# Weight matrices through GpSimd's transfer queue, late stores through SyncE's, in a gated linear attention with a max-of-three feed-forward layer

## The chip, the cores and the metric

The kernel runs on one core of a Trainium2 chip. The metric is the device time of one execution in microseconds. Engines are named as in the profile: PE (TensorE matmuls; PEld its weight loads), DVE (VectorE), ACT (ScalarE), POOL (GpSimd) and SP (SyncE). Three of them can issue transfers between memory and the on-chip buffer: SP, ACT and POOL; a transfer is then run by the core's 16 DMA engines. Each engine runs its own instructions in program order.

## The reference

```python
# q, k, v, alpha: (4, 8, 768, 48); w1, w2, w3: (384, 768); w_out: (768, 384)
for t in range(S):
    state = alpha[:, :, t, :, None] * state + np.einsum('bhd,bhe->bhde', k[:, :, t], v[:, :, t])
    y[:, :, t] = np.einsum('bhd,bhde->bhe', q[:, :, t], state)
x = y.transpose(0, 2, 1, 3).reshape(B * S, H * D)          # (3072, 384)
h = np.maximum(np.maximum(x @ w1, x @ w2), x @ w3)
out = h @ w_out                                            # (3072, 384), float32
```

## The kernel before

The sequence of 768 steps is cut into 6 blocks of 128. A **unit** u is one block of one of the 4 batches, with all 8 heads: 24 units, in the order block by block. Two units make a **pair** n (12 pairs): q, k, v and alpha are loaded for a pair at a time, or for one unit of it ("half loads", 192 KB) in pairs 0, 1 and 3.

For each unit, `decay` takes the logarithm of alpha on ACT (L509); `prep` sums it along the block on PE (L562), takes exp of plus and minus the sum on ACT (`ep`, `en`, L565 and L567), multiplies q and k by these on POOL or DVE (L574, by the table `EARLY`), scales v (L586), transposes q and k (on PE, L544, copied out by DVE, L548; from unit `CROSS_IN` on by a transfer of SP, L593), and computes scores (L608) that DVE masks (`LA`, L613). `output` multiplies the scores by v and the carried state by q (L654, L651), scales the result into `xb` on ACT (L662) and transposes it to `xT` (on PE, L676, copied by DVE, L680; from unit `CROSS_OUT` on by a transfer of SP). `state` carries the state to the next block (L706, L712, L719).

The feed-forward layer uses max(a, b, c) = a + max(0, b − a, c − a). With w1 as the base, `subs` computes `wd` = w2 − w1 and w3 − w1 in 16 bits (L456). For a group f of one or two units, `ffn` runs six (or four) pieces: x·wd on PE (L747), relu for the first matrix on ACT (L758), maximum for the second on DVE (L763). The output is h·w_out plus x·(w1·w_out) (L780); the product w1·w_out, `w1o`, is made once: `turned` transposes w1 on PE (L474) with copies on ACT (L480), and `folded` multiplies it by w_out (L491). That product is called the **fold** here. Groups 0 and 1 are single units (`SINGLE`), the others two units. Each finished unit is copied out of PSUM by ACT (L791) and stored by ACT's queue (L792).

The order is not that of the source: each step is handed to a planner (`Plan`) with its engine, a cost, a rank, what it reads and writes; `order` simulates the engines, the transfer queues and the PSUM banks and emits the steps engine by engine in the order found. Two lists stand outside of that: SP issues its loads in the order of `FIRST`, and then pair by pair, in one line ("loads"). In the kernel before, `FIRST` holds the weights too, in column parts of 512 and 256 (`WCUTS`), so SP's one queue brings both; `wload` (L437) lands w1 and w_out as 32-bit numbers in a staging buffer that they share (`ws0`), and ACT casts them to 16 bits (L447). `WARM` names zero matmuls on PE that stand beside the startup; before, their count is 0.

## Time and profile before

| | |
|---|---|
| three runs | 153.97, 154.49 (median), 156.53 us |
| profiled execution | 154.55 us, span 152.8 us, granted PE clock 1.00 |
| PE busy | 132.5 us (87%) |
| DVE, ACT, POOL busy | 97.7, 86.7, 66.7 us |
| transfers by SP's queue | 24.74 MB, 76.8% of 16 engines' span |
| transfers by ACT's queue | 4.72 MB, 9.1% |
| read from memory, written | 23.69 MB, 4.72 MB |

The span is the time from the first to the last instruction; the execution's own time is 1.75 us longer. "Busy" leaves out waits and the issuing of transfers. In the windows, each row is a stretch of the span: its bounds and length, then busy time and number of instructions of PE, PEld, DVE, ACT and POOL, the granted clock, the mean share of the 16 DMA engines, and GB/s. In the chain of waits each row is start, length and what the end of the program hung on then; a DMA in it is a wait for a transfer, from its issue to its landing. In the timeline a row is start, length, engine, line, operation and tiles, with the idle time ahead of it and what ended that in brackets.

### The profile page before, as it was taken

The page shows a single profiled execution, that of the slowest core. Times are in us where ns is not written, and L with a number is a line of the kernel's source. Part 1 is how long each engine was busy: PE and PEld are TensorE (multiplying, and loading weights), DVE is VectorE, ACT ScalarE, POOL GpSimd, SP SyncE. Part 2 cuts the span into 40 slices and gives each one's busy share as a digit, 9 for nine tenths or more (in the row PEclk, how much of TensorE's full clock was granted, in tenths as well). Part 3 has the DMA queues.
Part 4 walks back from the last instruction along what each step waited for, and adds up shares of the span by engine and source line. Part 5 has one row for each costly group of instructions (what it writes and reads, how often), then busy time and mean ns, then how long its engine had stood idle before and what let it go on. Part 6 is the DMA issues. An engine that isn't in the chain of part 4 may idle for free.

```text
span 152.8 us, 4049 instructions
## 1 busy us (share of the span) xinstructions
PE 132.5 (87%) x1616; PEld 104.4 (68%) x1616; DVE 97.7 (64%) x172; ACT 86.7 (57%) x173; POOL 66.7 (44%) x95
## 2 busy tenths in 40 slices
PE   0416458689999999999999999999999999999990
PEld 0205237558877887798697788698697878778760
DVE  7025552878793699988686799587874482385230
ACT  3706556658626785777748567568395426336211
POOL 0223107010721143587978589496999910000000
PEclk9999999999999999999999999999999999999999
DMA  6999998999799999999999979999999706020113
GB/s 121 203 275 195 283 342 186 375 221 238 162 230 206 274 235 193 241 263 197 223 245 219 230 174 221 193 282 180 257 213 221 193 4 172 0 101 6 66 37 103
DMA packets 110578, 29.71 MB, mean 194 GB/s; under 512 B 104160, under 2 KB 109408, under 8 KB 110560
## 3 DMA queue, kind: packets, MB, share of 16 engines
q1 hardware_dynamic: 106816, 24.74, 76.8%
q10 hardware_dynamic: 3744, 4.72, 9.1%
q8 instruction: 12, 0.20, 0.5%
q14 instruction: 6, 0.05, 0.1%
HBM read 23.69 MB, written 4.72 MB: 186 GB/s over the span
## 4 chain that ended last, share of the span: by engine, by line
PE 77%; SPq 11%; DMA 7%; ACT 2%; issue 1%; ACTq 0%
PE psum L747 30%; PE psum L780 23%; SPq L415 10%; PE psum L544 5%; DMA ws<-in_moe_w_out_dram 4%; PE psum L608 4%; DMA ws<-in_moe_w_dram 3%; PE psum L654 3%; PE psum L676 2%; PE psum L562 2%; PE psum L651 2%; PE psum L706 2%; PE psum L491 2%; PE psum L522 1%; ACT wo L447 1%
## 5 line engine op out<-in xcount | busy, mean ns | idle before, releaser
L747 PE MATMUL psum<-xT,wd 128*128 128x256 f16 (+1 forms) x468 | 55.5, 270 | 1.6 <-DVE xT L680 1.6
L747 PEld LDWEIGHTS <-wd 128*128 128x128 f16 x468 | 42.4, 101 | 7.1 <-DVE wd L456 1.6
L613 DVE TENSOR_TENSOR LA<-psum,c 128x1024 f16<-128x1024 f32 x24 | 28.6, 1219 | 7.7 <-PE psum L608 7.5
L758 ACT ACTIVATE hT<-psum 128x512 f16<-128x512 f32 (+1 forms) x37 | 21.5, 588 | 16.8 <-PE psum L747 15.9
L763 DVE TENSOR_TENSOR hT<-psum,hT 128x512 f16<-128x512 f32 (+1 forms) x37 | 24.5, 673 | 9.5 <-PE psum L747 9.3
L574 POOL TENSOR_TENSOR qk<-qn,ep 128x384 f16<-128x384 f32 x18 | 18.0, 998 | 23.0 <-ACT ep L565 12.8
L780 PE MATMUL psum<-wo,hT 128*128 128x384 f16 x144 | 27.3, 326 | 0.0
L791 ACT COPY ob<-psum 128x384 f32<-128x384 f32 x23 | 11.0, 479 | 18.8 <-PE psum L780 18.6
L574 POOL TENSOR_TENSOR qk<-kn,en 128x384 f16<-128x384 f32 x19 | 19.3, 1020 | 2.9 <-DMA kn<-in_k_dram 2.8
L780 PEld LDWEIGHTS <-hT 128*128 128x128 f16 x144 | 14.1, 98 | 9.3
L586 POOL TENSOR_SCALAR v<-vn,c 128x384 f16<-128x384 f32 x21 | 12.6, 602 | 17.4 <-DMA vn<-in_v_dram 17.3
L719 POOL TENSOR_TENSOR Z<-U,G 48x192 f16<-48x192 f32 x32 | 15.8, 502 | 9.0 <-DVE U L712 7.8
L662 ACT ACTIVATE xb<-psum,c 128x384 f16<-128x384 f32 x24 | 13.7, 581 | 6.7 <-PE psum L654 3.2
L548 DVE COPY qkT<-psum 128x1024 f16<-128x1024 f16 x20 | 13.6, 687 | 5.8 <-PE psum L544 5.7
L544 PE MATMUL psum<-c,qk 128*128 128x128 f16 x160 | 13.1, 228 | 3.5 <-POOL qk L574 3.5
L780 PE MATMUL psum<-w1o,xT 128*128 128x384 f16 x72 | 15.6, 326 | 0.0
L680 DVE COPY xT<-psum 128x384 f16<-128x384 f16 x24 | 8.3, 354 | 9.8 <-PE psum L676 8.2
L562 PE MATMUL psum<-la,c 128*128 128x384 f16 x24 | 8.4, 351 | 6.0 <-ACT la L509 6.0
L544 PEld LDWEIGHTS <-qk 128*128 128x128 f16 x160 | 10.5, 102 | 4.1 <-POOL qk L574 3.8
L565 ACT ACTIVATE ep<-psum 128x384 f32<-128x384 f32 x24 | 11.9, 494 | 1.8 <-PE psum L562 1.5
L509 ACT ACTIVATE la<-an 128x768 f16<-128x768 f32 (+1 forms) x14 | 10.4, 746 | 3.6 <-DMA an<-in_alpha_dram 3.6
L567 ACT ACTIVATE en<-psum 128x384 f32<-128x384 f32 x24 | 11.9, 497 | 0.4 <-ACT ob L791 0.4
(41 smaller groups left out, 147.0 us busy)
## 6 DMA issues: line engine op xcount, KB each, us to landing
out_dram<-ob ACTq DMA_DIRECT2D x23, 192.0 KB, 3.0
an<-in_alpha_dram SPq DMA_DIRECT2D x10, 384.0 KB, 5.6
qn<-in_q_dram SPq DMA_DIRECT2D x9, 384.0 KB, 6.5
kn<-in_k_dram SPq DMA_DIRECT2D x9, 384.0 KB, 6.5
vn<-in_v_dram SPq DMA_DIRECT2D x9, 384.0 KB, 6.0
ws<-in_moe_w_dram SPq DMA_DIRECT2D x3, 768.0 KB, 6.6
qn<-in_q_dram SPq DMA_DIRECT2D x6, 192.0 KB, 4.5
kn<-in_k_dram SPq DMA_DIRECT2D x6, 192.0 KB, 4.6
```

What stands on the lines that cost most here:

```text
L415: nc.sync.dma_start(t[:, lo:hi], views[x][cb * P:(cb + 1) * P, g * HG + lo:g * HG + hi])
L544: nc.tensor.transpose(live[tk][:, w, j, :], qk[:, w, 2 * j:2 * j + 2, :], ident)
L548: plan.step("DVE", 0.69, u, lambda: nc.vector.tensor_copy(out=qkT, in_=live[tk]), reads=[tk], writes=[("qkT", u % 3)])
L574: nc.gpsimd if eng == "POOL" else nc.vector).tensor_mul(
L586: lambda: nc.gpsimd.tensor_scalar(out=v16, in0=ld["v"][n % 5][:, hs], scalar1=vsc, scalar2=1.0, op0=AOP.mult, op1=AOP.mult),
L613: lambda: nc.vector.tensor_mul(LA.rearrange("p a b t -> p (a b) t"), live[Ak].rearrange("p a (b t) -> p (a b) t", t=P), maskA.unsqueeze(1) ...
L662: lambda: nc.scalar.activation(out=xb, in_=live[yk].rearrange("p a b -> p (a b)"), func=AFT.Copy, scale=ysc),
L719: eng.tensor_mul(Zn[rows, :, cols], U[rows, :, cols], G[rows, i * NP:(i + 1) * NP].unsqueeze(2).broadcast_to([D, NP, D]))
L747: nc.tensor.matmul(live[gk][:, jj, :], wd[:, kt, g, j * P:(j + 1) * P], xT[:, kt, :], start=(kt == 0), stop=(kt == NFT - 1))
L758: lambda h=h, gk=gk: nc.scalar.activation(out=h, in_=live[gk], func=AFT.Relu),
L763: lambda h=h, gk=gk: nc.vector.tensor_max(h, live[gk], h),
L780: nc.tensor.matmul(live[ok], a[:, i * P:(i + 1) * P], w, start=(kt == 0), stop=(kt == nk - 1))
```

## The change

The four weight matrices leave SP's list. POOL issues one transfer for each whole matrix (`weights`): w1 and w_out arrive as 16-bit numbers in `w1h` and `wo16`, cast by the transfer; w2 and w3 arrive as 32-bit numbers. `WPOOL` says behind what each is issued: w1 at the start, w2 when v of unit 0 is scaled, w3 and w_out when v of unit 1 is. The staging buffer and ACT's four casts are gone. The subtractions all run on DVE. Stores of units 16 to 22 are issued by SP instead of ACT (`LEAVE`). xT of units 18 to 23 is made by SP's transposing transfer (`CROSS_OUT` 24 to 18), and qk of unit 20 is transposed by PE again (`CROSS_IN` 20 to 21). 18 zero matmuls stand in the startup (`WARM`). The tables of the planner, `EARLY`, `LEAD`, `FIRST` and the queue constants are new, so that the order of all engines is another.

In the order that comes out, PE's first steps are: the sum for unit 1 (from here on lines are those of the changed kernel; L588), the 18 transpositions of w1 (L500), the sum for unit 0, the transpositions and scores of units 1 and 0; then 72 matmuls of the feed-forward groups 0 and 1 (L773, with qk of unit 3 in between), scores of unit 3, 12 matmuls of the fold (L517), qk of unit 2, the output of unit 3, and the last 6 of the fold. POOL's first steps are: the transfer of w1 (L467), k and q of unit 1, v of unit 0, q of unit 0, the transfer of w2, v of units 2 and 1, the transfers of w3 and w_out. SP's list begins with alpha and k of unit 1, alpha of unit 0, q of both, v and k of unit 0 and v of unit 2; then come k of units 2 and 3, alpha of unit 2 and, as the twelfth half load, v of unit 1.

```diff
--- before.py
+++ after.py
@@ -23,29 +23,29 @@
 HOP = {"PE": 0.25, "ACT": 0.1, "DVE": 0.1, "POOL": 0.1, "SP": 0.0}
 TURN_RANK, TURN_COST = 2.0, 0.1
 SP_FIRST = 0.9
-QUEUES = ("SP", "ACT")
-DMA_IN = {"SP": 0.9, "ACT": 0.9}
-DMA_OUT = {"SP": 0.9, "ACT": 0.9}
-DMA_BOTH = {"SP": 0.17, "ACT": 0.8}
-LANES, LANES_USED, LANDING = {"SP": 6, "ACT": 99}, 2, 2.4
+QUEUES = ("SP", "POOL")
+DMA_IN = {"SP": 0.9, "POOL": 2.7}
+DMA_OUT = {"SP": 0.9, "POOL": 0.9}
+DMA_BOTH = {"SP": 0.15, "POOL": 0.85}
+LANES, LANES_USED, LANDING = 6, 2, 2.4
 SPARE = 1.5
-LEAD = (9.0, 6.5, 2.0, 7.5)
-EARLY = {0: ("DVE", "DVE", "POOL"), 2: ("POOL", "DVE", "POOL"), 3: ("DVE", "DVE", "POOL"),
-         4: ("DVE", "POOL", "POOL"), 6: ("DVE", "DVE", "ACT"), 8: ("POOL", "POOL", "ACT"),
-         9: ("DVE", "DVE", "ACT"), 11: ("DVE", "POOL", "POOL")}
+LEAD = (8.0, 8.5, 2.0, 8.5)
+EARLY = {0: ("POOL", "DVE", "POOL"), 1: ("POOL", "POOL", "POOL"), 3: ("DVE", "POOL", "POOL"),
+         4: ("POOL", "POOL", "POOL"), 5: ("DVE", "POOL", "POOL"), 6: ("POOL", "POOL", "POOL"),
+         7: ("DVE", "POOL", "POOL"), 8: ("POOL", "DVE", "POOL"), 11: ("POOL", "POOL", "POOL")}
 WCUTS = (0, 512, 768)
-SUBS = {(1, 0): "DVE", (1, 1): "POOL", (2, 0): "DVE", (2, 1): "DVE"}
-FIRST = (("a", 0, 1, 2), ("a", 0, 0, 1), ("q", 0, 1, 2), ("k", 1, 0, 1), ("q", 0, 0, 1),
-         ("k", 0, 1, 2), ("w", 0, 0), ("v", 1, 0, 1), ("v", 0, 0, 1), ("k", 0, 0, 1),
-         ("k", 1, 1, 2), ("a", 1, 0, 1), ("w", 0, 1), ("v", 0, 1, 2), ("w", 1, 0), ("w", 1, 1),
-         ("w", 3, 1), ("aq", 1, 1, 2), ("q", 1, 0, 1), ("w", 3, 0), ("w", 2, 0), ("w", 2, 1),
-         ("v", 1, 1, 2), ("aqkv", 2, 0, 2), ("k", 3, 0, 1), ("a", 3, 0, 2), ("v", 3, 1, 2),
-         ("q", 3, 0, 1), ("v", 3, 0, 1), ("q", 3, 1, 2), ("k", 3, 1, 2))
-WARM = (-1, 1, 0)
-BACK, WQUEUE, WTAX = 1, "SP", 0.1
+SUBS = {(1, 0): "DVE", (1, 1): "DVE", (2, 0): "DVE", (2, 1): "DVE", (2, 2): "DVE",
+        (1, 2): "DVE"}
+FIRST = (("a", 0, 1, 2), ("k", 0, 1, 2), ("a", 0, 0, 1), ("q", 0, 1, 2), ("qv", 0, 0, 1),
+         ("k", 0, 0, 1), ("v", 1, 0, 1), ("k", 1, 0, 2), ("a", 1, 0, 1), ("v", 0, 1, 2),
+         ("a", 1, 1, 2), ("q", 1, 1, 2), ("q", 1, 0, 1), ("v", 1, 1, 2), ("aqkv", 2, 0, 2),
+         ("ka", 3, 0, 1), ("a", 3, 1, 2), ("q", 3, 0, 1), ("qv", 3, 1, 2), ("k", 3, 1, 2),
+         ("v", 3, 0, 1))
+WARM = (0, 1, 18)
+WPOOL, ROWS, WTAX = {0: (), 1: (0, "v"), 2: (1, "v"), 3: (1, "v")}, False, 0.1
 SINGLE, LAST = 2, 0
 PAIRS, WIDE = 10, 99
-CROSS_IN, CROSS_OUT = 20, 24
+CROSS_IN, CROSS_OUT, LEAVE = 21, 18, 16
 FETCH, FETCHES, STORE = 0.75, (25.0, 10.2), 0.25
 CLOCK_WINDOW, CLOCK_PHASE, CLOCK_WAKE, CLOCK_KEEP = 3.413, 0.0, 0.75, 0.4
 
...
@@ -422,43 +424,67 @@
                       late=0.0 if n < 3 else SPARE)
             asked.append((x, n % 5, lo // H))
 
-    nparts = len(WCUTS) - 1
+    nparts = 3 if ROWS else len(WCUTS) - 1
     matrices = (moe_w1, moe_w2, moe_w3, moe_w_out)
-    casting = {g: tuple(x[2] for x in FIRST if x[:2] == ("w", g)) for g in (0, 3)}
+    by_sp = {g: [x[2] for x in FIRST if x[:2] == ("w", g)] for g in (0, 3)}
+    got, built = set(), []
+
+    def arranged(g, part):
+        got.add((g, part))
+        for k, (h, what) in enumerate(((0, turned), (3, folded))):
+            if len(built) == k and all((h, p) in got for p in range(nparts)):
+                built.append(h)
+                what()
 
     def piece(t, g, part):
+        if ROWS:
+            return t[:, 2 * part:2 * part + 2, :] if g == 3 else t[:, part:part + 1, :]
         lo, hi = WCUTS[part], WCUTS[part + 1]
         return t[:, lo // P:hi // P, :] if g == 3 else t[:, :, lo:hi]
 
+    def size(part):
+        return DF if ROWS else NFT * (WCUTS[part + 1] - WCUTS[part])
+
     def wload(g, part):
-        room = [("ws room", p) for p in casting[0]] if g == 3 else []
-        gate = [asked[-1 - BACK]] if len(asked) > BACK and WQUEUE == "ACT" else []
-        plan.step(WQUEUE, 0.5, -1.0,
-                  lambda: (nc.scalar if WQUEUE == "ACT" else nc.sync).dma_start(
+        plan.step("SP", 0.5, -1.0,
+                  lambda: nc.sync.dma_start(
                       piece(wst[g], g, part),
                       piece(matrices[g].rearrange("(t p) f -> p t f", p=P), g, part)),
-                  reads=gate + room, writes=[("ws", g, part)],
-                  line="weights" if WQUEUE == "ACT" else "loads",
-                  load=3.25 * (WCUTS[part + 1] - WCUTS[part]) / DF
-                  + (WTAX if WQUEUE == "SP" else 0.0))
+                  reads=[("ws room", p) for p in by_sp[0]] if g == 3 else [],
+                  writes=[("ws", g, part)], line="loads",
+                  load=(3.15 if ROWS else 3.25) * size(part) / (NFT * DF) + WTAX)
         if g in (0, 3):
-            n = NFT * (WCUTS[part + 1] - WCUTS[part])
-            plan.step("ACT", 0.2 + 0.00083 * n, -0.5,
+            plan.step("ACT", 0.2 + 0.00083 * size(part), -0.5,
                       lambda: nc.scalar.copy(out=piece((w1h, 0, 0, wo16)[g], g, part),
                                              in_=piece(wst[g], g, part)),
                       reads=[("ws", g, part)],
                       writes=[("w", g, part)] + [("ws room", part)] * (g == 0))
+            arranged(g, part)
+
+    def weights(g, gate):
+        cast = g in (0, 3)
+        plan.step("POOL", 0.78, -1.0,
+                  lambda: nc.gpsimd.dma_start((w1h, wst.get(1), wst.get(2), wo16)[g],
+                                              matrices[g].rearrange("(t p) f -> p t f", p=P)),
+                  reads=gate, writes=[("w" if cast else "ws", g, p) for p in range(nparts)],
+                  line="weights", load=3.3)
+        if cast:
+            for p in range(nparts):
+                arranged(g, p)
 
     def subs(g, part):
-        cols = slice(WCUTS[part], WCUTS[part + 1])
-        n, eng = NFT * (cols.stop - cols.start), SUBS[g, part]
-        plan.step(eng, 0.2 + n * (0.0019 if eng == "POOL" else 0.00102), 0.0 if g == 1 else 3.0,
+        eng = SUBS.get((g, part), "DVE")
+        plan.step(eng, 0.2 + size(part) * (0.0019 if eng == "POOL" else 0.00102),
+                  0.0 if g == 1 else 3.0,
                   lambda: (nc.gpsimd if eng == "POOL" else nc.vector).tensor_sub(
-                      wd[:, :, g - 1, cols], wst[g][:, :, cols], w1h[:, :, cols]),
+                      piece(wd[:, :, g - 1, :], g, part), piece(wst[g], g, part),
+                      piece(w1h, g, part)),
                   mode=int(eng == "DVE"),
                   reads=[("ws", g, part), ("w", 0, part)], writes=[("wd", g, part)])
 
     def parts_of(j):
+        if ROWS:
+            return list(range(nparts))
         return [p for p in range(nparts)
                 if WCUTS[p] < 2 * (j + 1) * P and WCUTS[p + 1] > 2 * j * P]
 
@@ -769,6 +795,7 @@
             r = rank[2 * (NJ // span) + i]
             ok = ("op", m)
             nk = NFT + NJ
+            cb, b = divmod(m, B)
             parts = [(0, nk)] if m < NU - UB else [(0, nk - span), (nk - span, nk)]
             for lo, hi in parts:
                 def shrink(i=i, ok=ok, lo=lo, hi=hi):
@@ -791,8 +818,17 @@
                 nc.scalar.copy(out=obs[m % 4], in_=live[ok])
                 nc.scalar.dma_start(out[b * S + cb * P:b * S + (cb + 1) * P, :], obs[m % 4])
 
+            if m < min(LEAVE, NU - 1):
+                plan.step("ACT", 0.86, r, leave, reads=[ok], writes=[("ob room", m % 4)], load=-STORE)
+                continue
             if m < NU - 1:
-                plan.step("ACT", 0.86, r, leave, reads=[ok], writes=[("ob room", m % 4)], load=-STORE)
+                plan.step("ACT", 0.49, r,
+                          lambda m=m, ok=ok: nc.scalar.copy(out=obs[m % 4], in_=live[ok]),
+                          reads=[ok], writes=[("ob room", m % 4), ("ob", m)])
+                plan.step("SP", 0.4, r,
+                          lambda b=b, m=m: nc.sync.dma_start(
+                              out[b * S + cb * P:b * S + (cb + 1) * P, :], obs[m % 4]),
+                          reads=[("ob", m)], writes=[("left", m)], load=-STORE)
                 continue
             left, right = slice(0, DM // 2), slice(DM // 2, DM)
             rows = out[b * S + cb * P:b * S + (cb + 1) * P, :]
@@ -816,13 +852,14 @@
     for what, n, lo, *hi in FIRST:
         if what == "w":
             wload(n, lo)
-            if n in casting and lo == casting[n][-1]:
-                turned() if n == 0 else folded()
         else:
             load(n, lo * H, hi[0] * H, what)
     if WARM[0] < 0:
         warm(*WARM)
-    made = dict.fromkeys(SUBS, False)
+    for g, gate in WPOOL.items():
+        if not gate:
+            weights(g, [])
+    made = {(g, p): False for g in (1, 2) for p in range(nparts)}
     due = []
     for n in range(NU // B):
         us = list(range(n * B, (n + 1) * B))
@@ -839,13 +876,17 @@
                 state(u)
         for u in range(n * UB, (n + 1) * UB):
             prep(u)
+            for g, gate in WPOOL.items():
+                if gate and gate[0] == u:
+                    weights(g, [("v16", u % 7) if gate[1] == "v"
+                                else ("qk", u % 7, "qk".index(gate[1]))])
             if u >= PAIRS and u % UB == 0:
                 continue
             if u == WARM[0]:
                 warm(*WARM)
             for v in (u - 1, u) if u >= PAIRS else (u,):
                 output(v)
-        for key in SUBS:
+        for key in made:
             if not made[key] and ("w", 0, 0) in plan.writer and ("ws", *key) in plan.writer:
                 made[key] = True
                 subs(*key)
```

More of the change, by code (lines that the diff above doesn't have):

```diff
@@ L232, in order @@
                         t = max(t, held["DVE" if e == "POOL" else "POOL"])
-                    if self.steps[i][6] and len(lanes) >= LANES[e]:
-                        if lanes[-LANES[e]] is None:
+                    if e == "SP" and len(lanes) >= LANES:
+                        if lanes[-LANES] is None:
                             continue
-                        t = max(t, lanes[-LANES[e]])
+                        t = max(t, lanes[-LANES])
                     turn = TURN_RANK if e == "PE" and self.steps[i][7] != mode else 0.0
@@ L248, in order @@
                 end, i = dma.next(commit=True)
-                lanes[number[i]] = end
+                if i in number:
+                    lanes[number[i]] = end
                 self.landed[i] = end
@@ L270, in order @@
                 dma.add(e, t + cost + DMA_IN[e], load, i, late)
-                number[i] = len(lanes)
-                lanes.append(None)
+                if e == "SP":
+                    number[i] = len(lanes)
+                    lanes.append(None)
             else:
```

## The prediction

> **What bounds the kernel now.** First the head of the page, for the span and the busiest engine:
>
> ```profile
> span 152.8 us, 4049 instructions
> ...
> PE 132.5 (87%) x1616; PEld 104.4 (68%) x1616; DVE 97.7 (64%) x172; ACT 86.7 (57%) x173; POOL 66.7 (44%) x95
> ```
>
> The profiled execution took 154.55 us, 1.75 more than its span; the median of the three runs, 154.49, is the same within 0.1. A measurement of this kernel can tell about 2% (3.1 us) from no change. Then the windows of 8 us, for where PE is not busy:
>
> ```profile
> 0.00:8.00 8.00, 1.76 (x14) 0.97 (x14) 3.52 (x19) 4.02 (x8) 1.20 (x5) 1.00 0.85 161
> 8.00:16.00 8.00, 3.53 (x32) 2.84 (x33) 2.78 (x5) 2.97 (x3) 2.16 (x3) 1.00 0.98 234
> 16.00:24.00 8.00, 3.82 (x41) 2.62 (x41) 4.59 (x6) 4.10 (x8) 1.83 (x2) 1.00 1.04 304
> 24.00:32.00 8.00, 6.25 (x82) 5.33 (x80) 3.79 (x6) 5.33 (x10) 1.81 (x2) 1.00 1.00 300
> 32.00:40.00 8.00, 8.00 (x108) 6.35 (x107) 6.64 (x12) 5.66 (x13) 1.93 (x2) 1.00 1.06 195
> ```
>
> From 32 us on PE is busy for all of each window up to 144; before, it idles while the DMA engines are full (DMA share near 1). So there are two stages: a startup set by transfers, and a dense stage set by PE's work. The chain of waits shows where one passes into the other:
>
> ```profile
> 23.53 6.05 DMA ws<-in_moe_w_out_dram
> ...
> 29.60 1.48 ACT wo L447
> ...
> 31.12 1.14 PE psum L491 x6
> ```
>
> The second part of w_out lands at 29.58, ACT casts it, and from 31.12, the first matmul of the fold w1·w_out, PE never waits again until its last matmul starts at 148.8. That is 117.7 us; 4.0 more are the last copies and stores. Hence time = start of the fold + dense work + 4.0 + 1.75.
>
> **What the change takes from the dense work.** In PE's new order both halves of the first two FFN groups stand ahead of the fold; now the second halves (36 matmuls of 128 columns; nine take 0.51 in the chain) come after it: −2.0. Units 18 to 23 lose the transposition of xb on PE (three matmuls, 0.17 each in the chain): −1.0. Unit 20 goes back to PE for qk (eight matmuls, 0.45): +0.45. Unit 2's qk transposition and scores (0.45, 0.23) move behind the fold: +0.7. Sum −1.9, dense work 115.8. The 18 zero matmuls (WARM) lie in the startup, where PE waits anyway; six of them, cold, are 2 us at most if that wait were gone.
>
> **When can the fold start?** Its new gate is w_out as fetched by POOL's queue, the last of four fetches. No row shows a transfer issued by POOL, so I build it from neighbours:
>
> ```profile
> 2.25 1.67 DVE L381 MEMSET Z<- 128x192 uint32 x8
> ...
> 4.15 0.52 ACT L509 ACTIVATE la<-an 128x384 f16<-128x384 f32 x1 [1.24 <-DMA an<-in_alpha_dram]
> ...
> 5.10 0.52 ACT L509 ACTIVATE la<-an 128x384 f16<-128x384 f32 x1 [0.42 <-DMA an<-in_alpha_dram]
> ...
> 7.57 0.56 DVE L574 TENSOR_TENSOR qk<-qn,ep 128x384 f16<-128x384 f32 x1 [3.65 <-DMA qn<-in_q_dram]
> ```
>
> - Loads: the first lands at 4.15, and from 5.10 to 7.57 three more land: 0.82 us per half load (one unit of a, q, k or v).
> - A weight's transfer, X: the first 768 KB of w3 let DVE start at 31.66, 2.06 after w_out had let ACT start at 29.60; a whole matrix, half as large again, 3.1. That is the lower end (nothing beside it). If loads beside it get half of the bytes, 6.2. The issue table has ACT's 192 KB stores landing in 3.0 us while SP's loads of the same size take 4.5: a second queue does not stand behind the first. So I lie near the lower end: X = 3.9.
> - Rest of issue to landing: the 96.5 KB constant on ACT's queue took 2.5 us, the 1.5 KB one 3.2; with 1.0 for POOL's own work on the issue (its instructions take 0.6 to 1.0), 4.2. Bounds 2.5 and 6.
>
> w1: issued at about 0.7, landed at 0.7 + 4.2 + 3.9 = 8.8. PE's second step in program order is the 18 transpositions of w1, so unit 0 waits behind it: six transpositions 0.75 (twelve took 1.46), ACT's copy 0.75, ln 0.52, second copy 0.75, exp 0.48, POOL's multiply 0.99, about 4.5 with the hand-overs. Only behind that multiply does POOL issue w2: 13.3, landed 21.4. w3's issue stands behind v of unit 1, the twelfth half load: 4.15 + 11·0.82 = 13.2, and 3.3 more that w1's stream takes from it: 16.5. POOL scales it (0.6) and issues w3 and w_out at about 17.3 and 18, in time to queue behind w2: w3 lands at 25.3, w_out at 29.2. So landing = 13.6 + 4X, and the fold starts at 29.4 (no cast in between).
>
> What must be there by then: wd from w3, 1.76 + 0.95 on DVE, 28.0, and its 18 last matmuls, 29.0; 0.4 is left. Next is alpha of pair 2, half loads 17 and 18: 4.15 + 17·0.82 + 4·3.3 = 31.3, ln 0.84, 32.1; PE asks for it 3.8 after the fold starts (1.95 + 0.45 + 0.2 + 0.98 + 0.23), at 33.2. It is covered by 1.1 us; a still earlier fold would wait here.
>
> **Costs taken at nothing.** ACT loses 4.6 us of casts, three scalings and seven store issues (0.34 each), all idle time now. POOL gains 3 q, 3 k and 3 v operations (7.9 us) and four issues (2.4 to 4), and loses one subtraction (2.06): about 9 us, in units 0 to 11, where it was busy 7.0 of 32 us and 5.6 of the next 16; without that cover, qk of unit 3 or 4 would be late by 1 us each. SP's queue: the xb transfers of units 22 and 23 stand behind two stores, whose copies come earlier in ACT's order; after the last attention matmul PE has 18 + 24 matmuls of 256 columns (4.6) and 18 of w_out (2.9), 7.5 us, against copy 0.58, two issues of 1.25 and landing (qkT's transfers took 3.1 to 4.1): about 6. Margin 1.4; the price without it is 1 to 2 us. The last store's right half may wait up to 0.4 for SP's store before it.
>
> **Sum:** 29.4 + 115.8 = 145.2 for PE's last matmul, span 149.2, time 151.0: 1.7 from the earlier fold, 1.9 from the dense work. With X = 3.1 and 2.5 of latency, the fold could start at 26.4, but alpha would hold PE for 1.9 more: 149.9. The other end is the third rival.
>
> **Rivals.**
> 1. *The bytes set the startup, whoever issues them.* DMA share is already 0.98 to 1.04 from 8 to 32 us, and the bytes from memory are the same. Then the fold starts where it did, 31.1, or at 32.0 if w2's stream pushes v of unit 1 (16.5 against w2's start near 17) and w3 is issued behind it. Time 31.1 + 121.55 = 152.7, to 153.6. Against it: the cast ahead of the fold (1.48) goes, and the last part of w_out took 6.05 us from issue to landing for 768 KB that need 2.1, with loads of SP ahead of it in the one queue. The Trainium skill (DMA: Bandwidth & Descriptors, section Issuing engines are not separate DMA queues) says just this, that another issuer saves only issuing time. By that rule the time is this rival's; the DMA share agrees with it.
> 2. *w1's fetch starts late.* DVE fills tiles until 3.92. If POOL's issue is held until then, everything after w1 moves by 3.2: fold 32.6, time 154.2. No POOL work stands beside those fills in the trace. The Trainium skill (SBUF — State Buffer, section SBUF: two separate sides, the box on the "DVE blocks DMA" trap) says that POOL cannot write descriptors while DVE holds the shared port; no run here shows whether a fill does.
> 3. *Slower: POOL's transfers are slow and stand one behind the other.* X counts four times, and w1 holds PE, ACT and through unit 0 the issue of w2. The fold may start 1.9 later than before, at 33.0, until nothing is gained: 13.8 + 4X = 33.0 gives X = 4.8. At X = 6.2 (loads take half, or the two casting transfers run at half rate) w_out lands at 38.4: 38.6 + 121.55 = 160.1. For it: casts by transfer are in no row. Against it: the stores' 3.0.
>
> **How the numbers follow.** Forecast 0.43 (its own range 149.5 to 151.4), rival 1 0.17, rival 2 0.12, rival 3 0.28. Over 2% faster is below 151.4: the forecast, 0.43. Rivals 1 and 2 lie within 2%: 0.29. Rival 3 is mostly past 157.6: 0.28. The range goes from 149.0, just under the floor of 149.9, to 159.0, which leaves out the far end of rival 3, some 0.15, and 0.05 below.
>
> **What would show it.** Right: w1h landed at 8 to 9.5 us, w2 issued near 13, w3 landed near 25 to 26, the fold (L517) starting at 29 to 30 and PE without a gap from there, last matmul near 145. Rival 1: landing of w_out at 31 to 32. Rival 2: w1h landed near 12 with a normal transfer. Rival 3: a weight's transfer of 5 us and more, PE idle before L517. The step I trust least is X; wrong would also be any wait of PE in the dense stage, above all on alpha of pair 2 or on xT of units 22 and 23.

## The result and the profile after

The changed kernel takes 156.62 us (median of 20 runs, 155.99 to 158.81) against 154.79 for the kernel before (20 runs, 153.33 to 157.31). The ratio is 1.014, with an interval of 1.011 to 1.017: 1.4% slower, where 2.3% faster was forecast. Its profiled execution took 156.10 us with a span of 154.3 (1.5 more than before). Disturbed runs are left out of the ratios.

The head of the page first. PE is busy 2.0 us longer (the zero matmuls are in it) and POOL 11:

```profile
span 154.3 us, 4077 instructions
...
PE 134.5 (87%) x1624; PEld 104.4 (68%) x1624; DVE 96.9 (63%) x162; ACT 81.1 (53%) x167; POOL 78.1 (51%) x107
```

The windows, with the same columns and stretches as those of before:

```profile
0.00:8.00 8.00, 0.48 (x1) 0.10 (x1) 3.09 (x18) 2.68 (x4) 1.16 (x5) 1.00 0.87 156
8.00:16.00 8.00, 4.86 (x47) 3.73 (x47) 2.65 (x3) 3.54 (x7) 4.89 (x6) 1.00 1.02 201
16.00:24.00 8.00, 3.43 (x28) 2.19 (x29) 1.34 (x2) 2.39 (x5) 2.33 (x4) 1.00 1.03 266
24.00:32.00 8.00, 7.09 (x83) 5.14 (x82) 6.91 (x8) 3.59 (x8) 5.83 (x4) 1.00 1.11 258
32.00:40.00 8.00, 8.00 (x106) 5.82 (x104) 6.76 (x11) 3.92 (x10) 0.91 (x2) 1.00 1.01 197
```

The DMA engines are as full as before (the column before the last). The GB/s beside it are not to be compared with those of before: both kernels read 23.69 MB, but a casting transfer counts at its written size, so that the four matrices of 1.18 MB stand in POOL's queue as 3.54 MB. In the third row DVE works 1.34 us of 8, against 4.59 before, and PE 3.43: the engines wait while the DMA engines are full, so what is carried is not what is asked for. The chain of waits in that stretch (start, length, what the end hung on) shows when:

```profile
14.15 0.77 POOL ws L467
...
15.55 6.06 issue
...
22.30 0.48 PE psum L680 x8
...
30.03 1.76 DVE wd L479
...
31.83 2.19 PE psum L773 x36
```

POOL issues w2, scales v of unit 2, and then the chain stands still for 6 us. The timeline names the load that this gap waited for, and three places where PE stopped:

```profile
8.84 1.46 PE L500 MATMUL psum<-c,w1h 128*128 128x128 f16 x12 [3.78 <-DMA w1h<-in_moe_w_dram]
...
21.66 0.59 POOL L612 TENSOR_SCALAR v<-vn,c 128x384 f16<-128x384 f32 x1 [6.10 <-DMA vn<-in_v_dram]
22.19 0.79 POOL L467 DMA_DIRECT2D ws<-in_moe_w_dram  x1
...
22.30 0.48 PE L680 MATMUL psum<-v,LA 128*128 128x48 f16 x8 [4.01 <-POOL v L612]
...
31.83 2.19 PE L773 MATMUL psum<-xT,wd 128*128 128x128 f16 x36 [0.91 <-DVE wd L479]
...
34.28 1.96 PE L517 MATMUL psum<-wo,w1T 128*128 128x384 f16 x11
```

It is v of unit 1. SP asked for it at 14.17 us, 0.07 after POOL had begun to issue w2; it landed at 21.58, with w2 (21.63). Behind it stood POOL's issue of w3 (22.19) and w_out (22.98) and PE's next step (22.30). The fold starts at 34.28, 3.16 us later than before (31.12). The last matmul starts at 150.34, so the dense work is 116.06 us, 1.61 less than before. 3.16 − 1.61 = 1.55, the whole difference of the spans.

The matrices themselves came no later after their issue than forecast (7.5 us against 8.1). In the table of issues (KB each, us from issue to landing; the last one queued behind w3):

```profile
ws<-in_moe_w_dram POOLq DMA_DIRECT2D x2, 1152.0 KB, 7.5
...
w1h<-in_moe_w_dram POOLq DMA_DIRECT2D x1, 576.0 KB, 7.5
wo<-in_moe_w_out_dram POOLq DMA_DIRECT2D x1, 576.0 KB, 10.7
```

### The profile page after: what moved, and what is told of

The parts are those of the page before. It is cut to its first block, busy times and chain, and to the rows that moved or that the text cites. A ratio compares the mean times of both kernels' runs of the same rounds, so it can differ in the third digit from the quotient of the medians.

```text
span 154.3 us, 4077 instructions
## 1 busy us (share of the span) xinstructions
PE 134.5 (87%) x1624; PEld 104.4 (68%) x1624; DVE 96.9 (63%) x162; ACT 81.1 (53%) x167; POOL 78.1 (51%) x107
## 3 DMA queue, kind: packets, MB, share of 16 engines
q0 software_dynamic: 1600, 3.54, 8.9%
HBM read 23.69 MB, written 4.72 MB: 184 GB/s over the span
## 4 chain that ended last, share of the span: by engine, by line
PE 80%; SPq 5%; issue 5%; DVE 3%; DMA 2%; POOL 2%; ACT 0%; POOLq 0%; ACTq 0%; DVEq 0%
PE psum L773 30%; PE psum L807 23%; PE psum L570 5%; SPq L417 5%; PE psum L634 5%; PE psum L680 3%; PE psum L588 3%; DMA vn<-in_v_dram 2%; PE psum L677 2%; PE psum L732 2%; PE psum L702 2%; PE psum L517 2%; PE psum L714 2%; DVE wd L479 2%; PE psum L548 1%
## 5 line engine op out<-in xcount | busy, mean ns | idle before, releaser
L773 PE MATMUL psum<-xT,wd 128*128 128x256 f16 (+1 forms) x468 | 52.8, 264 | 0.9 <-DVE wd L479 0.9
L773 PEld LDWEIGHTS <-wd 128*128 128x128 f16 x468 | 41.3, 98 | 6.3 <-DVE wd L479 1.1
L600 POOL TENSOR_TENSOR qk<-qn,ep 128x384 f16<-128x384 f32 x21 | 21.7, 1032 | 25.4 <-ACT ep L591 24.3
L789 DVE TENSOR_TENSOR hT<-psum,hT 128x512 f16<-128x512 f32 (+1 forms) x37 | 24.3, 671 | 15.7 <-PE psum L773 12.7
L784 ACT ACTIVATE hT<-psum 128x512 f16<-128x512 f32 (+1 forms) x37 | 21.6, 589 | 18.4 <-PE psum L773 17.2
L600 POOL TENSOR_TENSOR qk<-kn,en 128x384 f16<-128x384 f32 x22 | 22.3, 1017 | 8.7 <-DMA kn<-in_k_dram 6.3
L574 DVE COPY qkT<-psum 128x1024 f16<-128x1024 f16 x21 | 14.4, 688 | 11.2 <-PE psum L570 10.9
L612 POOL TENSOR_SCALAR v<-vn,c 128x384 f16<-128x384 f32 x24 | 16.3, 681 | 7.5 <-DMA vn<-in_v_dram 7.4
L688 ACT ACTIVATE xb<-psum,c 128x384 f16<-128x384 f32 x24 | 13.8, 580 | 10.1 <-PE psum L680 7.2
L570 PE MATMUL psum<-c,qk 128*128 128x128 f16 x168 | 13.7, 228 | 1.5 <-DVE qk L600 1.2
L680 PE MATMUL psum<-v,LA 128*128 128x48 f16 x192 | 11.5, 186 | 4.0 <-POOL v L612 4.0
L818 ACT COPY ob<-psum 128x384 f32<-128x384 f32 x16 | 7.7, 478 | 13.0 <-PE psum L807 12.9
L680 PEld LDWEIGHTS <-LA 128*128 128x128 f16 x192 | 9.9, 98 | 5.0 <-issue 4.6
L588 PE MATMUL psum<-la,c 128*128 128x384 f16 x24 | 8.4, 352 | 5.1 <-ACT la L535 5.1
```

The costliest lines, as they stand in the source:

```text
L570: nc.tensor.transpose(live[tk][:, w, j, :], qk[:, w, 2 * j:2 * j + 2, :], ident)
L574: plan.step("DVE", 0.69, u, lambda: nc.vector.tensor_copy(out=qkT, in_=live[tk]), reads=[tk], writes=[("qkT", u % 3)])
L600: nc.gpsimd if eng == "POOL" else nc.vector).tensor_mul(
L612: lambda: nc.gpsimd.tensor_scalar(out=v16, in0=ld["v"][n % 5][:, hs], scalar1=vsc, scalar2=1.0, op0=AOP.mult, op1=AOP.mult),
L680: nc.tensor.matmul(yp[:, 2 * j + p, :], LA[:, p, j, :], v16[:, 2 * j + p, :], start=(cb == 0), stop=True, skip_group_check=True)
L688: lambda: nc.scalar.activation(out=xb, in_=live[yk].rearrange("p a b -> p (a b)"), func=AFT.Copy, scale=ysc),
```

## The experiments

Lines of code are those of the changed kernel, shifted by a few where an edit adds lines. "Fold" is the start of the first matmul w1·w_out in the profiled execution. The twelve runs at a glance; the ratio is to the kernel before, run on the same chip. Where a matrix is not fetched, it is not in the output either:

| run | edit | v of unit 1 landed | fold | median us | ratio (interval) |
|---|---|---|---|---|---|
| before | | 18.59 | 31.12 | 154.79 | 1 |
| after | | 21.58 | 34.28 | 156.62 | 1.014 (1.011–1.017) |
| e1 | v of unit 1 asked earlier | 15.62 | 37.29 | 160.78 | 1.036 (1.030–1.043) |
| e2 | w3, w_out issued right behind w2 | 26.16 | 39.36 | 161.82 | 1.046 (1.041–1.051) |
| e3 | xT of 18 to 23 on PE again | 21.23 | 36.69 | 157.85 | 1.023 (1.017–1.029) |
| e4 | before, with the late edits alone | 18.53 | 30.50 | 154.71 | 1.000 (0.996–1.004) |
| e5 | w2 issued behind v of unit 1 | 18.88 | 35.74 | 156.20 | 1.012 (1.007–1.018) |
| e6 | e1 and e5 together | 15.07 | 36.30 | 158.21 | 1.024 (1.017–1.031) |
| e7 | w3 not fetched | 22.26 | 35.41 | 157.02 | 1.017 (1.010–1.023) |
| e8 | before's parts, on ACT's queue | 21.70 | 34.73 | 160.01 | 1.038 (1.032–1.044) |
| e9 | w2, w3 in three transfers each | 20.52 | 34.43 | 156.68 | 1.012 (1.006–1.018) |
| e10 | no zero matmuls | 21.84 | 34.66 | 155.94 | 1.012 (1.006–1.017) |
| e11 | e7 and e10 together | 21.26 | 33.69 | 155.87 | 1.013 (1.008–1.018) |
| e12 | w2 not fetched | 17.77 | 30.06 | 152.38 | 0.987 (0.982–0.993) |

Each landing and fold is that of one profiled execution, and these took from 1.7 us less (e1) to 1.9 us more (e3) than their run's median. e3 has the startup of the changed kernel, and still its fold is 2.4 us later: w3 landed at 30.78 instead of 29.57, PE waited for its subtraction, and then the granted PE clock (the 0.50 in the window below) was halved, so that 36 matmuls took 3.81 us instead of 2.19:

```profile
32.62 3.81 PE L773 MATMUL psum<-xT,wd 128*128 128x128 f16 x36 [2.17 <-DVE wd L479]
```

```profile
32.90:36.30 3.40, 3.40 (x35) 3.29 (x31) 2.15 (x4) 0.00 (x0) 0.00 (x0) 0.50 0.80 158
```

So a difference of 1 or 2 us between two folds of the table says nothing by itself. The profiled executions of e5 and e6 also have 3.4 us at 0.50 behind a wait of PE.

**The late edits alone (e4), and one of them undone (e3).** e4 is the kernel before with its own startup, and only the stores from unit 16 on by SP, the transposed xT of units 18 to 23 and qk of unit 20 on PE. e3 is the changed kernel with xT on PE.

```diff
e4, in the kernel before:
-CROSS_IN, CROSS_OUT = 20, 24
+CROSS_IN, CROSS_OUT, LEAVE = 21, 18, 16
e3, in the changed kernel:
-CROSS_IN, CROSS_OUT, LEAVE = 21, 18, 16
+CROSS_IN, CROSS_OUT, LEAVE = 21, 24, 16
```

> The kernel before with the late part of the change alone: CROSS_OUT 18, CROSS_IN 21, stores of units 16 to 22 by SP; weights stay in SP's list. By PE's work: 1.0 us less and 0.45 more, 0.55 less than before, 154.2 against 154.8. Rival: the stores and transfers on SP's queue cost a wait, no gain or a loss.

> CROSS_OUT back to 24: xT of units 18 to 23 is again transposed on PE and copied by DVE; the startup is the same. If the dense stage is PE's work alone, as I hold, 1.0 us of matmuls come back: time 157.6, PE's last matmul 117.1 after the fold starts instead of 116.1. Rival: SP's transfers bring waits of their own that cost what they save: time 156.6 or less.

e4 is the same as before, 154.71. Its last matmul starts 0.6 earlier, but so does its fold; the dense work is 117.68 against 117.67. PE's work fell by 0.56 us, and a few small waits, the largest of 0.3 us for DVE's mask near 134 us, used it up. In e3 the dense work is 117.05 against 116.06: the 1.0 us of the forecast. So in the changed kernel the transposing transfers bring their full gain, and from the fold to the last matmul PE is busy for all of its 116.06 us. The stores were not tried apart from the rest. The loss lies in the startup.

**Other places for v of unit 1 (e1), for w3 and w_out (e2), for w2 (e5), and for both v and w2 (e6).** The steps are moved in the emitted order, and nothing else is.

```diff
     seq, where = plan.order()
e1: +    v1 = marks["v", 0, 1]                      # SP's load of v of unit 1
    +    seq.remove(v1); seq.insert(seq.index(marks["k", 1, 0]), v1)
e2: +    for g in (3, 2):                           # w_out, w3
    +        i = marks["w", g]
    +        seq.remove(i); seq.insert(seq.index(marks["w", 1]) + 1, i)
e5: +    w2 = marks["w", 1]
    +    seq.remove(w2); seq.insert(seq.index(marks["w", 2]), w2)
e6: e1 and e5
```

> Only SP's order is changed: the load of v for unit 1 stands ahead of the load of k for units 2 and 3. Theory A (v of unit 1 is caught behind w2's stream, and POOL's issue of w3 and PE both wait for it): v of unit 1 lands near 15 instead of 21.58, w3 is issued near 16 instead of 22.19 and lands near 25.5 instead of 29.57, w_out near 29.4 instead of 33.71, the fold starts at 29.5 to 30.5 instead of 34.28, time about 152.3 (4.3 less). Theory B (the bytes moved set the startup, whatever the order): the fold moves by under 1 us, time 155.6 or more.

> Only POOL's order is changed: w3 and w_out are issued right behind w2, ahead of the scalings of v of units 2 and 1. Theory A: the three matrices stream without a hole, w3 lands near 25.5 and w_out near 29.4, but v of unit 1 still lands near 21.6, so that PE's wait for it (4 us) stays and DVE comes to w2's subtraction at 24.8 as before; loads of pair 1 are starved until 29, among them q of unit 3, which stands ahead of w3's subtraction on DVE. The fold starts at 32 to 34, time 154.5 to 156.5. Theory B: the bytes are the same, fold at 34, time 156.6. A rival within A, that the hole in POOL's stream alone is the loss: fold at 30.5, time 152.8.

> Only POOL's order is changed: w2 is issued behind the scalings of v of units 2 and 1, right ahead of w3 and w_out. Theory C (while POOL's queue streams a matrix, some 3.6 us, SP's loads nearly stop; what decides is which loads lie behind the stream that PE's fixed order asks for): all loads of pair 1 up to q land by 21, v of unit 1 near 17, w2 is issued near 18 and lands near 25.5, w3 29, w_out 33; w3's subtraction ends near 32, the fold starts at 33, time 155.4 (1.2 less than the changed kernel). Theory A as first held (only v of unit 1 matters): the same 155.4. Theory D (the second stall, DVE and POOL slowing each other at 28 to 33 us): 156.6, since that work stays.

> Both moves: v of unit 1 ahead of k of units 2 and 3 in SP's list, and w2 issued behind the scaling of v of unit 1. Theory C: v of unit 1 lands near 15, w2 is issued near 16.2 and lands near 23.7, w3 27.3, w_out 31.1; alpha of both units of pair 1 and q of unit 3 land ahead of w2's stream, near 18 to 20; the rest of pair 1 only behind the streams. The fold starts near 31.3, time 153.5. Rival: one of the loads of pair 1 that PE or DVE need is still behind the stream, as in the run with v alone moved; then the fold is at 35 or more, time 158 or more.

e1 put v of unit 1 at 15.62, w3 at 25.35 and w_out at 29.19, nearly the landings of the forecast, and took 160.78 us where theory A said 152.3. The timeline of its PE shows the next load in the same place:

```profile
22.28 0.48 PE L590 MATMUL psum<-la,c 128*128 128x384 f16 x1 [4.81 <-ACT la L537]
```

Alpha of unit 2, asked at 13.88, now landed at 21.68 (16.57 in the changed kernel), alpha of unit 3 at 27.51, q of unit 3 at 29.55. In e2, with three matrices in a row, v of unit 1 itself landed at 26.16, not near 21.6 as expected, PE waited 8.2 us for it, and no theory had a time near 161.82. In e5 all loads of the first two pairs landed by 22.9, and w2 was late instead (27.30): PE idled 3.7 us for its subtraction, and w_out landed at 34.71; its time is not told apart from that of the changed kernel. In e6 v was early and w2 at 22.73; the load that stood behind the stream was q of unit 3. DVE's timeline:

```profile
29.98 0.56 DVE L603 TENSOR_TENSOR qk<-qn,ep 128x384 f16<-128x384 f32 x1 [3.52 <-DMA qn<-in_q_dram]
30.46 3.42 DVE L482 TENSOR_TENSOR wd<-ws,w1h 128x1536 f16<-128x1536 f32 x2
```

w3 had landed at 25.82, but DVE's program holds qk of unit 3 ahead of its subtraction. This is the rival that was written down for e6 (158 or more). Four placements, four different late transfers: each is slower than before, because in each of these orders DVE or PE asks soon for something that a stream holds up.

**How much the loads get beside a stream.** The queues' packets in stretches in which both had work (queue, packets, MB, share of 16 engines). First e2 from 19 to 23 us, w3 and w_out behind w2 on POOL's queue (q0), loads on SP's (q1):

```profile
q0 software_dynamic: 266, 1.54, 95.1%
q1 hardware_dynamic: 260, 0.05, 6.1%
```

Packet for packet the two queues get the same, 266 and 260. But POOL's packets hold 5.8 KB each on average (1.54 MB / 266; the large ones are 6144 bytes and take about 260 ns), and SP's one row of 48 numbers, 192 bytes in 15 ns. So the loads got 0.05 MB in 4 us, 12 GB/s; with SP alone in the queues (21.7 to 24.5 us in the changed kernel) they moved 0.53 MB in 2.8 us, 190 GB/s. SP's queue does not slow to a half or a fifth beside these weights, but to 6%.

One for one is not a fixed share. Where a stream sets in or ends SP gets more, and beside w1 it got one packet to six, from 4.5 to 6.5 us in the changed kernel, though three loads had been asked for that landed at 8.37, 9.50 and 10.27:

```profile
q0 software_dynamic: 233, 0.36, 108.4%
q1 hardware_dynamic: 37, 0.01, 2.9%
```

Why the share can lie below one to one, no run here shows.

**Is it POOL's queue (e8)?** The kernel before, replanned, with its weight parts on ACT's queue.

```diff
-BACK, WQUEUE, WTAX = 1, "SP", 0.1
+BACK, WQUEUE, WTAX = 1, "ACT", 0.1
```

> The kernel before with its weights issued by ACT's queue instead of SP's, in the same column parts, each held until the load before last has landed (the order is planned anew for that). If loads starve beside any second queue, and not beside POOL's alone, SP's loads show the same near standstill while a part streams, shorter ones (2 us for a part of 768 KB), and the same bytes have moved by 32 us; time 155 to 157. Rival: a queue of the hardware's own shares evenly and the fold comes earlier: 153.

The loads starve there too: PE waits 4.7 us at 8 and 4.5 at 18, and the kernel takes 160.01, more than either theory said. The queues from 9 to 10.5 us, ACT's being q10, with packets of 2 KB:

```profile
q10 hardware_dynamic: 268, 0.55, 94.0%
q1 hardware_dynamic: 94, 0.02, 5.8%
```

The loads get 12 GB/s here, one packet to three; over the two microseconds from 16 to 18, with packets of 1 and 2 KB, the counts are 386 and 392 and the loads get 35 GB/s. So SP's loads also starve beside a queue that is not POOL's. The whole 3.8% cannot be put down to that: the order of all engines was planned anew, the fold is 3.6 us later than before, and the dense work 2.8 us longer, 2.1 of it waits of PE.

**Smaller packets (e9).** w2 and w3 land in blocks of 128 columns with 4 columns between them, as three transfers per matrix:

```diff
-    wst = {g: sb.tile([P, NFT, DF], FP32, name=f"ws{g}") for g in (1, 2)}
+    wst = {g: sb.tile([P, NFT, DF // P, P + 4], FP32, name=f"ws{g}") for g in (1, 2)}
...
+            rows = matrices[g].rearrange("(t p) (c f) -> t p c f", p=P, f=P)
+            for t in range(NFT):
+                nc.gpsimd.dma_start(wst[g][:, t, :, :P], rows[t])
```

> Edit: order and gates of the changed kernel, but w2 and w3 land in blocks of 128 columns with 4 columns of padding between them, so that no packet of theirs is over 512 bytes (in the changed kernel they are 6144 bytes); each comes as three transfers instead of one. Theory T (the 16 DMA engines take one packet of each queue in turn, whatever its size): in the changed kernel, between 18 and 20 us, POOL's queue had 121 data packets of 6144 bytes (248 ns each) and SP's 180 of 192 bytes (16 ns each), so SP was left with 3 to 6% of the bytes. With 512-byte packets (about 30 ns, between the 16 ns of 192 bytes and the 50 ns of 1024) the packets stay one to one, but SP gets 192 of 704 bytes, 27%: some 67 GB/s beside the stream. v of unit 1, asked at 14.2, lands at 19 to 20.5 instead of 21.58; w2's own stream takes about 7 us instead of 3.6 and lands at 24 to 25.5. The wait of PE for v of unit 1 shrinks by 1 to 2 us, a wait for w2's subtraction takes its place, and w3 and w_out land at 30 to 31.5 and 34 to 36: 156 to 158. Theory U (SP's queue stands behind a second queue whatever the packets, or the memory is the limit): SP moves less than 30 GB/s beside the stream again, and v of unit 1 lands when w2 does, at 21.5 or later.

The edit did not do what it was meant to: the packets became 4096 bytes, not 512, so the 27% were not tried. v of unit 1 landed 1.1 us earlier, because POOL's queue stood empty between its transfers (from 18 to 19 us SP moved 1141 packets), and the last third of w2 2.4 us later (24.00); the time is that of the changed kernel. It lies in the range that was expected, but not for that reason. Beside w3 in three transfers SP got next to nothing from 25 to 27.5 us, 8 packets to 208, though a load asked for at 20.19 did not land until 33.84. But w_out's transfer, which casts, has small packets in any case (0.29 MB / 370 = 0.8 KB, counted as written), and here they met SP's loads from 29 to 31 us:

```profile
q0 software_dynamic: 370, 0.29, 90.8%
q1 hardware_dynamic: 372, 0.07, 32.9%
```

370 to 372: one for one at a second packet size, and the loads get 35 GB/s instead of 12.

**Bytes, or their place (e7, e12).** Two kernels with the same bytes left out, one matrix: in e7 w3, whose stream comes behind v of unit 1, in e12 w2, whose stream stands ahead of it. In e12 w2's subtraction reads 16-bit numbers and takes 1.8 us instead of 2.7.

```diff
e7:  + lambda: None if g == 2 else nc.gpsimd.dma_start((w1h, ...
     + ... piece(wst[1], g, part)                      # in the subtraction, for both
e12: + lambda: None if g == 1 else nc.gpsimd.dma_start((w1h, ...
     + ... piece(wst[g] if g == 2 else w1h, g, part)   # in the subtraction
```

> The changed kernel without the transfer of w3: its subtraction reads w2's tile, so that the third matrix is left out; all else and the order are the same. Theory C: w_out takes w3's place in the stream, issued at 22.2 and landed near 29.6 instead of 33.7; DVE's four subtractions follow one another from 24.8 to 30.3; the fold starts near 31.1, time 153.4: the startup gives back what one matrix's stream takes. Theory D (DVE and POOL slow each other, bytes do not matter): the subtractions still end near 33 and the time stays at 156.

> Edit: the changed kernel without the transfer of the second matrix (its subtraction takes w1 from itself, in 16 bits, at the same place; the second matrix is not in the output). It is the counterpart of the run without the third matrix, which moved as many bytes fewer, was fetched behind v of unit 1, and took 157.02 with its fold at 35.41. Theory C (what costs is that w2's stream stands ahead of v of unit 1 and the loads behind it, which PE's and POOL's orders wait for): with that stream gone, v of unit 1, asked at 14.2, lands at 16.5 to 17, alpha and q of unit 3 and q of unit 2 by 21, w3 is issued at 17.3 to 17.6 and lands at 25 to 25.5, w_out at 28.5 to 29.5; PE's wait at 17.8 goes, the feed-forward starts at about 23.4 instead of 28.30, its second half waits for w3's subtraction (25 to 28), and the fold starts at 29 to 29.7, which is the startup that the forecast worked out: last matmul at about 145.5, time 151.0 to 152.0. Theory D (bytes alone: one matrix less is 3.6 us of transfer less wherever it is): the same for both runs, so nothing here either, 156 to 157. Between them, 153 to 154.5, if the chain from v of unit 1 on holds a second wait that is hidden behind the first.

e7 gained nothing (157.02, where theory C said 153.4); e12 took 4.2 us off the changed kernel (152.38) and is the one run that beats the kernel before, though with one matrix less. Theory D of e12, bytes alone, is out: it gave both runs the same time. So is theory D of e7, that DVE and POOL slow each other: in e12 they do so as in the changed kernel (1.35 us for DVE's qk of unit 3, 2.47 for POOL's v). POOL's and PE's timeline of e12:

```profile
17.85 0.58 POOL L612 TENSOR_SCALAR v<-vn,c 128x384 f16<-128x384 f32 x1 [3.24 <-DMA vn<-in_v_dram]
18.38 0.81 POOL L467 DMA_DIRECT2D ws<-in_moe_w_dram  x1
...
18.49 0.48 PE L680 MATMUL psum<-v,LA 128*128 128x48 f16 x8 [0.38 <-POOL v L612]
...
24.16 2.17 PE L773 MATMUL psum<-xT,wd 128*128 128x128 f16 x36
...
27.62 2.19 PE L773 MATMUL psum<-xT,wd 128*128 128x128 f16 x36 [0.84 <-DVE wd L479]
...
30.06 2.12 PE L517 MATMUL psum<-wo,w1T 128*128 128x384 f16 x12
```

From PE's first use of v of unit 1 to the fold it is 30.06 − 18.49 = 11.6 us here, 34.28 − 22.30 = 12.0 in the changed kernel and 35.41 − 22.98 = 12.4 in e7, where w3's landing could not hold anything. e2, e10 and e11 have 12.5, 12.1 and 11.7. So when nothing else comes late the fold follows v of unit 1 by about 12 us; it is 13 to 17 where w2, alpha or q came late too (e1, e5, e6, e9) or w3 and the clock did (e3). Of the 4.2 us that e12 gains, 3.8 are the earlier landing of v of unit 1 and 0.4 the shorter way from there. In between lie, in the order of PE and DVE: the outputs of units 1 and 0 and their transpositions, w2's second subtraction behind the copy of unit 0's xT, qk of unit 3, w3's subtractions, both halves of the feed-forward. In e7 DVE's subtraction for the missing matrix began at 30.85, no earlier than with it:

```profile
28.87 0.36 DVE L706 COPY xT<-psum 128x384 f16<-128x384 f16 x1 [1.68 <-PE psum L702]
...
30.85 2.92 DVE L479 TENSOR_TENSOR wd<-ws,w1h 128x1536 f16<-128x1536 f32 x2
```

**The zero matmuls (e10), and with w3 left out as well (e11).** Twelve of the 18 stand in that chain of 12 us.

```diff
     seq, where = plan.order()
+    seq = [i for i in seq if i not in warms]
```

> Edit: the changed kernel with the 18 zero matmuls left out as the steps are emitted; every other step stays where it was on its engine. In the changed kernel 6 of them (25.67 to 27.2 us, at the low clock) stand ahead of the transposition of unit 0's output and 6 more (27.33 to 28.3) ahead of the first feed-forward matmuls. Theory C (PE's chain behind v of unit 1, with what stands in it, and then w3's landing): the transposition comes at about 26.2 instead of 27.16, the feed-forward starts at about 26.9 instead of 28.30, w2's second subtraction ends about 1 us earlier; but w3 lands at 29.57, its two subtractions end at 32.2 instead of 32.95, and the fold starts at about 33.6 instead of 34.28: 156.0, -0.6. Rival W (the zero matmuls raise the clock for the feed-forward behind them): without them its 36 matmuls take up to 4 us instead of 2.17, and the time is 156.6 to 158.

> Edit: both, the 18 zero matmuls left out and the transfer of the third matrix left out (its subtraction reads w2's tile instead, so that the third matrix is not in the output). The run without the third matrix alone took 157.02, its fold at 35.41, 1.68 us of DVE's idle time ahead of unit 0's transposed output and 2.92 us of subtraction behind that. Theory C: with the zero matmuls gone too, the chain behind v of unit 1 (22.3) is PE, the copy at about 27, w2's second subtraction to 28.2, the two for w3 to 31.1, the second feed-forward half 29.8 to 32.0, and the fold starts at 32.3 to 32.6: 153.9 to 154.5, about -2.7. If the bytes of the third matrix and the zero matmuls both cost nothing of the start, it stays at 156.5 to 157; if the clock is lower without the zero matmuls, 155 to 156.5.

The first feed-forward matmuls start earlier without them (26.83 instead of 28.30), and then run at half the rate. The line of e10, and under it that of the changed kernel:

```profile
26.83 4.02 PE L775 MATMUL psum<-xT,wd 128*128 128x128 f16 x36 [0.25 <-DVE wd L480]
```

```profile
28.30 2.17 PE L773 MATMUL psum<-xT,wd 128*128 128x128 f16 x36
```

What they cost ahead, 1.5 us, they save behind, 1.85. e10's median is 0.7 under that of the changed kernel, as theory C said, but not by its way: the 4.02 us are those of rival W, and the profiled fold is 0.4 later, not 0.7 earlier. The ratios of the two (1.012 and 1.014) are not told apart, so whether the zero matmuls pay is not settled; in either case they are not the loss. In e11 the 36 matmuls also took 4.02 us, and its 155.87 (154 was forecast by the main theory, 155 to 156.5 by its rival) fits the rival on PE's rate.

No run of a whole kernel beats the kernel before by more than its interval; e4 is the nearest, with a ratio of 1.000.

## Why the prediction was wrong, step by step

- **Start of the fold: 29.4 forecast, 34.28 measured.** This is the term that failed, 4.9 of the 5.1 us between the forecast and the profiled execution.
- *v of unit 1 at 16.5.* This is the step of it that failed. It landed at 21.58, 5.1 later. The estimate took 3.3 us from it for w1's stream and nothing for w2's, whose packets were thought to begin near 17. They began at 16.33. Without that stream it lands at 17.77 (e12), 1.3 later than worked out, because SP could only ask at 13.8 to 14.2. So the load was on the wrong side of the stream by about 1.4 us, and the price of that is the whole stream: 3.8 us that the sum put at nothing. Behind it the times held: from its landing to the fold 12.9 us were forecast and 12.7 measured.
- *What must be there by the fold.* That these 12.7 us came out is in part luck. The sum let the fold wait for w_out and for w3's subtraction (28.0) alone, and w_out, issued at 22.98, did land late, at 33.71. But PE and DVE reach w3's subtraction only through unit 0's output, which stands behind v of unit 1, and that second chain of 12 us was not in the sum. Both hang on the same load and end within 0.6 us of each other; the second ends last. e7, with neither w3 nor its stream, shows that the second alone can hold the fold: w_out landed at 31.59 there, and the fold started at 35.41.
- *X = 3.9, "near the lower end".* The size was about right: w3 landed 3.1 to 3.6 us after w2 where they followed each other (e1, e2, e5, e6), w_out 3.8 to 4.8 after w3. What it was taken to mean was wrong. The quick stores of ACT beside SP's loads were read as a favoured second queue; the other side of that row, what is left for SP, was not asked. It is 6% (e2), where a share between a fifth and a half had been reckoned with.
- **Rival 1, second form** (w2's stream pushes v of unit 1, w3 is issued behind it) was the mechanism. Its price, fold at 32.0, was too small by 2.3: it lies 2.6 us behind the forecast, less than one stream, where v of unit 1 was 5.1 later.
- **Rival 2** did not happen: w1's packets began 2.5 us behind its issue, against 2.2 and 2.4 for w2 and w3, which have no fills beside them. That it landed at 8.79 (8.8 forecast) is two misses that cancel: it was issued 0.55 later and took 0.6 less. **Rival 3** had the sign, and a range that holds the measured fold, but not the reason: a matrix with nothing ahead of it took 7.4 to 7.5 us from issue to landing (8.1 forecast), and the streams were not slow but too strong.
- **Dense work: 115.8 forecast, 116.06 measured.** From the fold on, 36 matmuls of the first groups are gone (2.0 us, as forecast) and the 18 transpositions of xb (1.0); qk and scores of units 2 and 20 add 1.2, as forecast. Added to the kernel before, the late edits' 0.56 of PE's work went into small waits (e4).
- **Costs taken at nothing** were nothing here: PE has no wait in the dense stage. For alpha of pair 2 that is no proof: it landed at 34.04, not 31.3, and with a fold at 29.4 PE would have asked for it at 33.2, before its logarithm (0.84) was done. As it landed here, only the late fold covered it.

The Trainium skill (DMA: Bandwidth & Descriptors, section Issuing engines are not separate DMA queues) was weighed in the prediction as a rule by which the startup would stay where it was. The trace agrees that all issuers share the same 16 engines: in e2 the shares of POOL's and SP's queues add up to 101%. It does not agree that another issuer changes only the time of issuing: the changed kernel and e8 move the weights to another issuer, and while these stream SP's loads get 0 to 6% of the engines' time in the stretches shown with packets of 1.5 KB and more, which makes them late.

## What to carry to other kernels

Before a large transfer is moved to a second queue, list the small loads that will be asked for while it streams, and ask for each which engine has it next in its program order: such a load is late by up to the rest of the stream, so it must be asked for well before or not be needed until after. Follow the gate of a late stage through the program order of every engine, not only to the landing of its own operand: here a matrix could be left out with no gain. When the transfer engines are full and the waits are for data, another issuer can move the wait to another load, as it did in every kernel here that fetched all matrices through a second queue; the order of the bytes has to follow the order of use, and one queue, as in the kernel before, brings them in the order of its list.

## What was not expected of the hardware

- In the midst of a stream of larger packets SP's loads get about one packet for one or fewer, not byte for byte: 266 to 260 with 6144 and 192 bytes (e2), 370 to 372 with 768 and 192 (e9), and fewer elsewhere, 233 to 37 beside w1, 268 to 94 beside ACT's 2 KB (e8) and 208 to 8 beside w3 in three transfers (e9). So the larger the neighbour's packets, the smaller is the most that the loads get of the bytes. The Trainium skill (DMA: Bandwidth & Descriptors, section Queues, rings and completion order) says that each engine goes round its queues in turn by packets; the equal counts agree, and the lower ones it does not explain. What a packet of 512 bytes beside the loads would do was not tried.
- A transfer that casts 1.18 MB to 16 bits took 0.2 to 1.5 us longer in the same run than one that does not: 3.8 us behind w3 in e1, where w3 took 3.6 behind w2, and 4.6 against 3.1 in e6. That is not the price of the cast alone, as its smaller packets also leave SP's loads more.
- DVE and POOL are slower while both work: in the changed kernel DVE's qk of unit 3 took 1.35 us instead of 0.55 beside POOL's qk (1.71 instead of 1.0), and POOL's v, beside DVE's subtractions, 2.47 instead of 0.6.
- PE's 36 matmuls took 4.02 us in e10, where PE had worked 3.1 of the 4.8 us ahead of them, and 2.17 in the changed kernel, where it had worked 6.0 of 6.3. The granted clock of e10's 4.02 us is given as 1.00, and that of the 3.81 us in e3 as 0.50. So a 1.00 in that column does not show the full rate in the startup, and a load that comes late can cost more than PE's wait for it.
